# Softcap attention and soft mixture of experts on one core: 24 instead of 13 joined tanhs, 95 instead of 93 tiles of exponentials on VectorE, and the work of each period placed anew

## The chip, the cores and the metric

The kernel runs on one core of one Trainium2 chip. The metric is the device time of one execution in microseconds (us), of which three runs are given. A profile of one execution gives start and length of each instruction on five engines: TensorE (PE, with its weight loads as PEld), VectorE (DVE), ScalarE (ACT), GpSimd (POOL) and SyncE (SP). Each engine executes its own list of instructions in order; between engines, semaphores hold an instruction back until what it needs is there.

## The reference

An attention with capped scores feeds a soft mixture of experts. Batch 8, 12 heads, 448 tokens, head size 64; 8 experts with 4 slots each, 1024 hidden units.

```python
scores = cap * np.tanh(q @ k.T / sqrt(64) / cap)          # cap = 30
attn = np.exp(scores - scores.max(-1)); attn /= attn.sum(-1)
x = (attn @ v)  ->  (3584, 768)
logits = x @ phi                                          # 3584 x 32
slot_input = softmax(logits, over tokens).T @ x           # 32 x 768
slot_out[e] = relu(slot_input[e] @ w1[e]) @ w2[e]
out = softmax(logits, over slots) @ slot_out
```

## The kernel before

The scores of two heads of a batch (a "pair", `pr` in the code, 48 in all) are worked off in 7 tiles of 448 queries by 64 keys of each head, the two heads one above the other in the 128 partitions. The 336 tiles go through the kernel in 56 chunks of 6 tiles. The main loop has one period `j` for each chunk (`for j in range(NCH)`).

- **Scores** (`qk_chunk`): TensorE writes three tiles, a half chunk, into three PSUM banks with 12 small matmuls in two groups of 6.
- **Tanh** (`tanh_chunk`): ScalarE reads scores from PSUM and writes 16-bit values into the buffer `ex` of the chunk (five of them, taken in turn). Usually one instruction takes three tiles (L366), so each half of the score buffer is free again as soon as its own tanh has ended. For a period in the list `JOINED`, one instruction takes all six tiles (L362). TensorE then can't write the scores of the next chunk before all of it has ended; so in such a period `qk_chunk(2j+2)` stands behind the products of the period, not among them.
- **Exponential** (`exp_chunk`): ScalarE turns the tanhs of the chunk before into exponentials (L374). In the chunks of the dictionary `SHARED`, the first one to three tiles are done by VectorE instead: `poly_exp` computes them in seven steps, numbered 0 to 6 (L602, L604 to L609; the steps 2, 4 and 5 have two operands in memory). The table `POLY` says in which period, and at which of its places, each step of each chunk stands.
- **Products** (`pv_first`, `pv_tail`, `pv_rest`): in period `j`, TensorE multiplies the exponentials of a pair that ends in chunk `j-2` with the values, and VectorE divides by the sums (`norm`: L634 `rec`, L637 `xq`). There is one PSUM bank for them (pool `psV`).
- **Side work**: queries and keys of four heads are loaded by GpSimd's queue (`load`), transposed by TensorE (`transp`) and copied to SBUF by VectorE (L281); finished rows are transposed (`x_transp`) and copied (L689). Logits, their exponentials, slot sums and transposes follow for each batch (`logits`, `e_exp`, `slot_sums`, `e_transp`, `e_sums`). All these transposes and sums use the one PSUM buffer of the pool `psT`: a transpose waits until VectorE has copied out the one before. GpSimd also builds the block of values (`vcast`, L289) and issues the loads of the expert weights.

Within a period the places are called 0, m, e, a, b, r, c and d, each with a place just ahead (`<a`) and just behind (`>a`). The helper `at(j, place, function, ...)` books a piece of work, and `run(j, place)` emits it there. `WHEN` holds the places of the side work. Before, it has 22 entries, each with an offset in periods from the start of a batch (`PER` = 7 periods), so that all batches run alike.

After the last period come the exponentials of the last chunk, the last two pairs with their transposes (`TAILSEQ`), and then the experts (`layer1`, `layer2`) and the output.

Of the kernel before, what the change touches and what calls it, by code (L numbers as in the profile page):

```python
# [37 lines left out]
def kernel(  # L38
# [337 lines left out]
    def exp_chunk(j):  # L376
# [4 lines left out]
    JOINED = (10, 14, 17, 21, 24, 28, 29, 31, 35, 38, 42, 45, 49)  # L381
    SHARED = {1: (2, 0), 3: (3, 0), 4: (3, 0), 6: (2, 0), 7: (3, 0), 9: (3, 0), 11: (3, 0), 12: (3, 0), 14: (3, 0), 16: (3, 0), 18: (3, 0), 19: (3, 0), 21: (3, 0), 23: (3, 0), 25: (3, 0), 26: (3, 0), 28: (3, 0), 30: (3, 0), 32: (3, 0), 33: (3, 0), 35: (3, 0), 37: (3, 0), 39: (3, 0), 40: (3, 0), 42: (3, 0), 44: (3, 0), 46: (3, 0), 47: (2, 0), 48: (2, 0), 49: (3, 0), 51: (2, 0), 52: (1, 0), 53: (3, 0), 54: (1, 0)}
    POLY = {(1, 'm'): ((1, 0),),
            (1, 'e'): ((1, 1),),
            (1, '>a'): ((1, 2),),
            (1, '>b'): ((1, 3),),
            (1, '>d'): ((1, 4),),
            (2, 'r'): ((1, 5),),
            (3, 'e'): ((3, 0),),
            (3, '<a'): ((3, 1), (1, 6)),  # L390
            (3, '<b'): ((3, 2),),
            (3, '>c'): ((3, 3),),
            (4, '<a'): ((3, 4),),
            (4, '>a'): ((3, 5),),
            (4, '<c'): ((4, 0),),
            (5, 'e'): ((4, 1), (3, 6)),
            (5, '<a'): ((4, 2),),
            (5, '>b'): ((4, 3),),
            (5, '>c'): ((4, 4),),
            (6, 'e'): ((6, 0), (4, 5), (6, 1)),  # L400
            (6, '<a'): ((4, 6),),
            (6, '>d'): ((6, 2),),
            (7, 'm'): ((6, 3),),
            (7, 'e'): ((7, 0),),
            (7, '>a'): ((6, 4),),
            (7, '<b'): ((6, 5),),
            (7, '<d'): ((7, 1),),
            (8, '0'): ((7, 2), (7, 3)),
            (8, '>b'): ((6, 6), (7, 4)),
            (8, '>c'): ((7, 5),),  # L410
            (9, 'm'): ((9, 0),),
            (9, '<a'): ((7, 6),),
            (9, '>b'): ((9, 1),),
            (9, '>d'): ((9, 2),),
            (10, 'e'): ((9, 3),),
            (10, '>b'): ((9, 4),),
            (10, '>d'): ((9, 5),),
            (11, 'e'): ((11, 0),),
            (11, '<a'): ((9, 6),),
            (11, '>a'): ((11, 1),),  # L420
            (11, '>b'): ((11, 2),),
            (11, '<c'): ((11, 3),),
            (11, '>c'): ((11, 4),),
            (12, '<a'): ((12, 0),),
            (12, '<b'): ((11, 5),),
            (12, '<c'): ((12, 1),),
            (12, '>d'): ((11, 6),),
            (13, '<b'): ((12, 2),),
            (13, '>b'): ((12, 3),),
            (13, '>c'): ((12, 4),),  # L430
            (13, '>d'): ((12, 5),),
            (14, '<a'): ((14, 0), (12, 6), (14, 1)),
            (14, '<d'): ((14, 2), (14, 3)),
            (15, '>a'): ((14, 4),),
            (15, '>d'): ((14, 5),),
            (16, 'm'): ((14, 6),),
            (16, 'e'): ((16, 0),),
            (16, '<b'): ((16, 1),),
            (16, '>d'): ((16, 2),),
            (17, 'm'): ((16, 3),),  # L440
            (17, '<a'): ((16, 4),),
            (17, '>d'): ((16, 5),),
            (18, 'e'): ((18, 0),),
            (18, '>a'): ((16, 6), (18, 1)),
            (18, '>b'): ((18, 2),),
            (19, '0'): ((18, 3), (18, 4)),
            (19, 'e'): ((18, 5),),
            (19, '<a'): ((19, 0),),
            (19, '<c'): ((18, 6),),
            (19, '>c'): ((19, 1), (19, 2)),  # L450
            (20, '>b'): ((19, 3),),
            (20, '>d'): ((19, 4),),
            (21, '>a'): ((19, 5), (19, 6)),
            (21, '<b'): ((21, 0), (21, 1)),
            (21, '>c'): ((21, 2),),
            (21, '<d'): ((21, 3),),
            (22, '>b'): ((21, 4),),
            (22, '<d'): ((21, 5),),
            (23, 'm'): ((21, 6),),
            (23, '<a'): ((23, 0),),  # L460
            (23, '>a'): ((23, 1),),
            (23, '>d'): ((23, 2),),
            (24, 'e'): ((23, 3), (23, 4)),
            (24, '>d'): ((23, 5),),
            (25, 'm'): ((23, 6),),
            (25, '<a'): ((25, 0), (25, 1)),
            (25, '>b'): ((25, 2),),
            (25, '<c'): ((25, 3),),
            (25, '>d'): ((25, 4),),
            (26, '0'): ((25, 5),),  # L470
            (26, '<b'): ((25, 6),),
            (26, '<c'): ((26, 0),),
            (26, '>d'): ((26, 1),),
            (27, '>a'): ((26, 2),),
            (27, '>b'): ((26, 3), (26, 4)),
            (28, 'e'): ((26, 5), (28, 0)),
            (28, '<a'): ((26, 6),),
            (28, '>b'): ((28, 1),),
            (28, '>c'): ((28, 2),),
            (29, '>a'): ((28, 3),),  # L480
            (29, '<b'): ((28, 4),),
            (29, '>d'): ((28, 5),),
            (30, 'm'): ((28, 6),),
            (30, '>a'): ((30, 0),),
            (30, '>c'): ((30, 1),),
            (31, '0'): ((30, 2),),
            (31, 'm'): ((30, 3),),
            (31, '<b'): ((30, 4),),
            (31, '<c'): ((30, 5),),
            (32, 'e'): ((32, 0),),  # L490
            (32, '<b'): ((30, 6), (32, 1)),
            (32, '>b'): ((32, 2),),
            (32, '<c'): ((32, 3),),
            (32, '>c'): ((32, 4),),
            (33, 'e'): ((33, 0),),
            (33, '<b'): ((32, 5),),
            (33, '<c'): ((33, 1),),
            (34, '0'): ((33, 2),),
            (34, 'e'): ((33, 3),),
            (34, 'r'): ((33, 4),),  # L500
            (34, '<c'): ((32, 6),),
            (35, '0'): ((33, 5),),
            (35, '<a'): ((33, 6),),
            (35, '<b'): ((35, 0),),
            (35, '>b'): ((35, 1),),
            (35, '<c'): ((35, 2),),
            (36, '<a'): ((35, 3),),
            (36, '>a'): ((35, 4),),
            (37, 'm'): ((35, 5), (35, 6)),
            (37, 'e'): ((37, 0),),  # L510
            (37, '<a'): ((37, 1),),
            (38, 'm'): ((37, 2),),
            (38, '>a'): ((37, 3),),
            (38, '>b'): ((37, 4),),
            (38, '>c'): ((37, 5),),
            (39, 'e'): ((37, 6),),
            (39, '>a'): ((39, 0), (39, 1)),
            (39, '>b'): ((39, 2),),
            (39, '<c'): ((39, 3),),
            (39, '>c'): ((39, 4),),  # L520
            (40, 'e'): ((40, 0),),
            (40, '<b'): ((40, 1),),
            (40, '>b'): ((39, 5),),
            (40, '>c'): ((40, 2),),
            (41, '<b'): ((40, 3),),
            (41, 'r'): ((40, 4),),
            (41, '<d'): ((39, 6),),
            (42, 'm'): ((40, 5),),
            (42, '<a'): ((42, 0),),
            (42, '>a'): ((40, 6), (42, 1)),  # L530
            (43, 'e'): ((42, 2), (42, 3)),
# [284 lines left out]
    for b in range(B):  # L816
        j, p = b * PER, 6 * b

        def when(nm):
            return j + WHEN[nm][0], WHEN[nm][1]  # L820

# [413 lines left out]
```

## Time and profile before

| what | value |
|---|---|
| time, median of 3 runs | 281.53 us (281.47 to 281.86) |
| span of the profiled execution | 279.2 us |
| median time less that span | 2.3 us |
| PE busy | 247.0 us, 88% |
| DVE busy | 239.1 us, 86% |
| ACT busy | 248.6 us, 89% |
| POOL busy | 142.0 us, 51% |
| granted TensorE clock, mean | 0.985 |

The page names no separate time for the profiled execution; only its span is given. The median stands 2.3 us above it. A row of a timeline gives start, length, engine, line and operation, output and inputs, shapes and count; in brackets stands the idle time of the engine ahead of it and what ended that. ScalarE and VectorE overlap the end of one instruction with the start of the next, so the step from one start to the next start tells what an instruction costs. The last period begins at 228.4 us, the experts at 239.6 us, and the last store ends with the span.

### The profile page before, as it was taken

The page shows a single profiled execution, that of the slowest core. Times are in us where ns is not written, and L with a number is a line of the kernel's source. Part 1 is how long each engine was busy: PE and PEld are TensorE (multiplying, and loading weights), DVE is VectorE, ACT ScalarE, POOL GpSimd, SP SyncE. Part 2 cuts the span into 40 slices and gives each one's busy share as a digit, 9 for nine tenths or more (in the row PEclk, how much of TensorE's full clock was granted, in tenths as well). Part 3 has the DMA queues.
Part 4 walks back from the last instruction along what each step waited for, and adds up shares of the span by engine and source line. Part 5 has one row for each costly group of instructions (what it writes and reads, how often), then busy time and mean ns, then how long its engine had stood idle before and what let it go on. Part 6 is the DMA issues. An engine that isn't in the chain of part 4 may idle for free.

```text
span 279.2 us, 10421 instructions
## 1 busy us (share of the span) xinstructions
PE 247.0 (88%) x4560; PEld 166.6 (60%) x4560; DVE 239.1 (86%) x473; ACT 248.6 (89%) x195; POOL 142.0 (51%) x198
## 2 busy tenths in 40 slices
PE   8898989998999999989999999899999999998720
PEld 7555556756675766566756675657566678553300
DVE  3479999999999999999999999999999997347940
ACT  4999999999999999999999999999999998237720
POOL 8796548662957296728673758375743230200000
PEclk9999999999999999999999999999999999999995
DMA  6999999999999999999999999999999588979997
GB/s 197 277 193 202 219 219 234 229 221 219 224 225 220 219 229 226 225 217 229 223 226 212 213 219 231 218 210 215 231 217 215 117 279 293 367 290 383 434 424 312
DMA packets 57340, 68.08 MB, mean 244 GB/s; under 512 B 4048, under 2 KB 53840, under 8 KB 56784
## 3 DMA queue, kind: packets, MB, share of 16 engines
q0 software_dynamic: 42448, 35.31, 80.0%
q1 hardware_dynamic: 14704, 32.02, 32.6%
q8 instruction: 35, 0.57, 0.7%
q10 hardware_dynamic: 144, 0.10, 0.1%
q14 instruction: 9, 0.07, 0.1%
HBM read 91.72 MB, written 19.27 MB: 398 GB/s over the span
## 4 chain that ended last, share of the span: by engine, by line
ACT 38%; DVE 27%; PE 27%; issue 3%; POOL 1%; ACTq 0%; DVEq 0%
ACT ex L366 15%; ACT ex L374 15%; PE pv L627 8%; ACT ex L362 6%; DVE xq L637 4%; PE sc L349 3%; DVE xp L605 3%; DVE xp L607 3%; DVE ex L608 2%; DVE ex L602 2%; PE so_ps L1098 2%; PE hp L1070 2%; DVE xf L604 2%; DVE ex L609 2%; DVE xp L606 2%
## 5 line engine op out<-in xcount | busy, mean ns | idle before, releaser
L366 ACT ACTIVATE ex<-sc 128x1344 f16<-128x1344 f32 (+1 forms) x87 | 112.9, 1402 | 0.9 <-PE sc L349 0.9
L374 ACT ACTIVATE ex<-ex 128x1344 bf16<-128x1344 f16 (+5 forms) x58 | 110.7, 1916 | 0.1
L627 PE MATMUL pv<-vbd,ex 128*128 128x130 bf16 (+1 forms) x1610 | 94.0, 212 | 7.6 <-POOL vbd L289 3.4
L627 PEld LDWEIGHTS <-ex 128*128 128x128 bf16 (+1 forms) x1680 | 75.6, 101 | 34.9 <-issue 6.2
L289 POOL CAST vbd<-vraw 64x896 bf16<-64x896 f32 x46 | 47.3, 1028 | 57.3 <-PE pv L627 35.7
L349 PE MATMUL sc<-qT,kT 64*64 64x448 bf16 x672 | 66.0, 359 | 6.7 <-ACT ex L366 4.8
L362 ACT ACTIVATE ex<-sc 128x2688 f16<-128x2688 f32 x13 | 33.6, 2586 | 0.0
L349 PEld LDWEIGHTS <-kT 64*64 64x64 bf16 x672 | 22.1, 105 | 16.3 <-ACT ex L366 6.9
L637 DVE TENSOR_TENSOR xq<-pv,rec 128x448 bf16<-128x448 f32 x46 | 28.7, 625 | 1.6
L607 DVE TENSOR_TENSOR xp<-xp,xf 128x1344 f16<-128x1344 f16 (+2 forms) x34 | 27.1, 798 | 0.6
L608 DVE TENSOR_TENSOR ex<-ex,xp 128x1344 uint16<-128x1344 uint16 (+2 forms) x34 | 26.9, 791 | 0.2
L605 DVE TENSOR_TENSOR xp<-xf 128x1344 f16<-128x1344 uint16 (+2 forms) x34 | 26.8, 789 | 0.2
L116 POOL DMA_DIRECT2D w1b<-in_moe_w_dram x32 | 26.3, 825 | 0.0
L602 DVE TENSOR_SCALAR ex<-ex 128x1344 uint16<-128x1344 f16 (+2 forms) x34 | 17.0, 500 | 1.4 <-ACT ex L366 0.8
L606 DVE TENSOR_SCALAR xp<-xp 128x1344 f16<-128x1344 f16 (+2 forms) x34 | 17.2, 505 | 0.6
L281 DVE COPY kT<-kps 128x896 bf16<-128x896 bf16 x23 | 14.2, 617 | 4.0 <-PE kps L276 2.8
L297 POOL MEMSET vbd<- 64x1 bf16 x22 | 2.8, 129 | 28.6 <-PE pv L627 28.3
L604 DVE TENSOR_SCALAR xf<-ex 128x1344 uint16<-128x1344 uint16 (+2 forms) x34 | 16.7, 491 | 0.4
L185 POOL DMA_DIRECT2D qb<-in_q_dram x22 | 16.3, 740 | 1.2 <-PE qps L279 0.5
L609 DVE TENSOR_SCALAR ex<-ex 128x1344 uint16<-128x1344 uint16 (+2 forms) x34 | 16.4, 483 | 0.4
L120 POOL DMA_DIRECT2D w2d<-in_moe_w_dram x21 | 16.4, 816 | 0.0
L185 POOL DMA_DIRECT2D kb<-in_k_dram x22 | 16.3, 739 | 0.0
(124 smaller groups left out, 320.2 us busy)
## 6 DMA issues: line engine op xcount, KB each, us to landing
w1b<-in_moe_w_dram POOLq DMA_DIRECT2D x32, 384.0 KB, 10.2
vraw<-in_v_dram SPq DMA_DIRECT2D x44, 224.0 KB, 6.2
w2d<-in_moe_w_dram POOLq DMA_DIRECT2D x21, 384.0 KB, 9.9
w2t<-w2d SPq DMA_DIRECT2D x21, 384.0 KB, 6.2
qb<-in_q_dram POOLq DMA_DIRECT2D x22, 224.0 KB, 8.2
kb<-in_k_dram POOLq DMA_DIRECT2D x22, 224.0 KB, 8.1
w2b<-in_moe_w_dram POOLq DMA_DIRECT2D x11, 384.0 KB, 9.5
out_dram<-ob SPq DMA_DIRECT2D x2, 1536.0 KB, 7.7
```

What stands on the lines that cost most here:

```text
L116: pool.dma_start(out=w1b[e][:, js, fs], in_=w1r[:, e, js, fs])
L185: pool.dma_start(out=t, in_=quad_ap(nm, Q))
L289: pool.tensor_copy(vbds[Q % 2][r, :, :, c0:c0 + DH], raw[r])
L349: ins = pe.matmul(sc[cs, u, 0:S], qkT["k", Q][r, c, cs], qkT["q", Q][r, :, cs], start=True, stop=True).ins
L362: apart["t", i - 1] = apart["t", i] = act.activation(exs[j].bitcast(F16), own["board"][:, :, 0:S], ACT.Tanh, scale=qk_scale / cap).ins
L366: ins = act.activation(exs[j][:, half * CS + u0:half * CS + u1, :].bitcast(F16), (own[0] if i == u0 == 0 else sc)[:, u0:u1, 0:S], ACT.Tanh ...
L374: act.activation(exs[j][:, u0:u1, :], exs[j][:, u0:u1, :].bitcast(F16), ACT.Exp, scale=cap)
L605: lambda: dve.tensor_tensor(p, s, s.bitcast(F16), op=ALU.mult),
L607: lambda: dve.tensor_tensor(p, p, s, op=ALU.mult),
L608: lambda: dve.tensor_tensor(y, y, p, op=ALU.add),
L627: pe.matmul(out_, exs[j][r, u, q0:q0 + (HP if tail else P)], v_, start=(c == 0 and g == gs[0] < NF), stop=(c == NT - 1), skip_group_check= ...
L637: dve.tensor_tensor(xq[Q][:, h, s0:s1, :], pv[:, 0:s1 - s0, 0:DH], rec.to_broadcast([P, s1 - s0, DH]), op=ALU.mult)
```

## The change

Four tables are replaced, and the loop that books the side work reads the new one. Nothing else is edited; the amount of work on TensorE stays, and so do the fill-in matmuls.

- `JOINED` has 24 periods instead of 13. The first is 5 instead of 10.
- `SHARED` has 34 chunks as before. Chunks 1, 52 and 54 have one tile more on VectorE (3, 2 and 2), chunk 39 one less (2), and chunk 45 takes the place of chunk 46. That makes 95 tiles instead of 93.
- `POLY` places almost all of the 238 steps anew.
- `WHEN` has an entry for each load, transpose, copy, logit and sum of each batch, without a common pattern.

```diff
-    JOINED = (10, 14, 17, 21, 24, 28, 29, 31, 35, 38, 42, 45, 49)
-    SHARED = {1: (2, 0), 3: (3, 0), 4: (3, 0), 6: (2, 0),
...
+    JOINED = (5, 7, 8, 10, 12, 14, 16, 17, 19, 21, 22, 24, 26, 28, 29, 31, 33, 35, 36, 38, 42, 43, 45, 49)
+    SHARED = {1: (3, 0), 3: (3, 0), 4: (3, 0), 6: (2, 0),
...
-            (54, '<b'): ((54, 0), (53, 5)),
-            (54, '>b'): ((54, 1),),
-            (54, '>c'): ((53, 6),),
-            (55, '0'): ((54, 2),),
-            (55, 'e'): ((54, 3),),
...
+            (54, '<c'): ((54, 2), (53, 6)),
+            (54, '>c'): ((54, 3), (54, 4)),
+            (55, 'm'): ((54, 5),),
+            (55, '<a'): ((54, 6),)}
...
-    WHEN = {'k1': (0, 'm'), 'q1': (0, 'b'), 'v1': (3, 'c'), 'k2': (2, 'a'), 'q2': (2, 'd'), 'v2': (7, 'b'),
...
+    WHEN = {'k1': (1, '0'), 'q1': (1, '0'), 'lk2': (2, 'c'), 'lq2': (0, 'e'), 'k2': (2, 'b'), 'q2': (1, 'd'),
...
+            'q23': (52, '0'), 'x21': (54, 'd')}
...
-        for n in (2, 3):
-            quad_in(3 * b + n, *(when(f"{x}{n}") for x in ("lk", "lq", "k", "q", "v")))
+        for Q in range(max(3 * b + 1, 2), min(3 * b + 4, NQ)):
+            quad_in(Q, *(WHEN.get(f"{x}{Q}", (NCH - 1, "e")) for x in ("lk", "lq", "k", "q")), None)
...
-            at(*when(f"x{hq}"), x_transp, NQB * b + hq)
+            at(*WHEN[f"x{NQB * b + hq}"], x_transp, NQB * b + hq)
```

The diff makes the new kernel's line numbers in these functions two lower (L689 becomes L687) and those behind the tables 13 higher (L1070 becomes L1083).

**ScalarE, chunks 1 to 7.** Each `ex<-sc` is a tanh, of three tiles (128x1344) or joined (128x2688), each `ex<-ex` an exponential; a minus stands for before, a plus for the change:

```order
 L366 ACTIVATE ex<-sc 128x1344 x2
-L374 ACTIVATE ex<-ex 128x1792
+L374 ACTIVATE ex<-ex 128x1344
 L366 ACTIVATE ex<-sc 128x1344 x4
 L374 ACTIVATE ex<-ex 128x2688
 L366 ACTIVATE ex<-sc 128x1344 x2
 L374 ACTIVATE ex<-ex 128x1344
-L366 ACTIVATE ex<-sc 128x1344 x2
+L362 ACTIVATE ex<-sc 128x2688
 L374 ACTIVATE ex<-ex 128x1344
 L366 ACTIVATE ex<-sc 128x1344 x2
 L374 ACTIVATE ex<-ex 128x2688
```

The exponentials of chunk 1 lose a tile to VectorE, and the tanh of chunk 5 is one instruction instead of two.

**VectorE, end of period 54 and period 55, before.** `ex_5289` is chunk 53, `ex_5394` chunk 54; `xps_5462` holds the transposed rows of pairs 42 and 43, `xps_5505` those of pair 44:

```order
L634 RECIPROCAL rec_5456<-pv_5399 128x7
L637 TENSOR_TENSOR xq_5398<-pv_5399,rec_5456 128x448
L689 COPY xT_5461<-xps_5462 128x896
L609 TENSOR_SCALAR ex_5289<-ex_5289 128x1344
L605 TENSOR_TENSOR xp_155<-xf_154 128x448
L606 TENSOR_SCALAR xp_155<-xp_155 128x448
L607 TENSOR_TENSOR xp_155<-xp_155,xf_154 128x448
L689 COPY xT_5504<-xps_5505 128x448
L608 TENSOR_TENSOR ex_5394<-ex_5394,xp_155 128x448
L609 TENSOR_SCALAR ex_5394<-ex_5394 128x448
L634 RECIPROCAL rec_5537<-pv_5490 128x7
L637 TENSOR_TENSOR xq_5398<-pv_5490,rec_5537 128x448
```

**The same place with the change.** Here `ex_5268` is chunk 53, `ex_5338` chunk 54, `xps_5452` the pairs 42 and 43, and `xps_5486` pair 44:

```order
L632 RECIPROCAL rec_5435<-pv_5380 128x7
L635 TENSOR_TENSOR xq_5379<-pv_5380,rec_5435 128x448
L603 TENSOR_TENSOR xp_155<-xf_154 128x896
L607 TENSOR_SCALAR ex_5268<-ex_5268 128x1344
L604 TENSOR_SCALAR xp_155<-xp_155 128x896
L605 TENSOR_TENSOR xp_155<-xp_155,xf_154 128x896
L687 COPY xT_5451<-xps_5452 128x896
L606 TENSOR_TENSOR ex_5338<-ex_5338,xp_155 128x896
L607 TENSOR_SCALAR ex_5338<-ex_5338 128x896
L687 COPY xT_5485<-xps_5486 128x448
L632 RECIPROCAL rec_5516<-pv_5471 128x7
L635 TENSOR_TENSOR xq_5379<-pv_5471,rec_5516 128x448
```

The copy of the pairs 42 and 43 stood right behind `xq` and now stands behind four steps of exponentials; the steps of chunk 54 have two tiles instead of one.

More of the change, by code (lines that the diff above doesn't have):

```diff
@@ L490 @@
[L490 to L499 removed]
+            (26, 'e'): ((25, 5),),
+            (26, '>b'): ((26, 0),),
+            (26, '<d'): ((26, 1),),
+            (27, 'm'): ((26, 2), (26, 3)),
@@ L572 @@
[L572 to L583 removed]
+            (40, 'm'): ((39, 4), (40, 0)),
```

359 lines of the change are left out of this document (179 added, 180 removed), and 25 rows, old and new, of the table WHEN.

## The prediction

> **What bounds the kernel now.** I read the page first, then the busy time by stretches of the main loop, then the timelines of ScalarE, TensorE and VectorE where they meet.
>
> ```profile
> span 279.2 us, 10421 instructions
> PE 247.0 (88%) x4560; PEld 166.6 (60%) x4560; DVE 239.1 (86%) x473; ACT 248.6 (89%) x195; POOL 142.0 (51%) x198
> ...
> 20.00:205.00 185.00, 171.19 (x3396) 118.38 (x3396) 177.89 (x339) 184.99 (x131) 115.59 (x155) 1.00 1.24 221
> 205.00:230.00 25.00, 23.46 (x456) 16.64 (x453) 24.54 (x57) 25.00 (x20) 7.67 (x11) 1.00 0.94 204
> ```
>
> The columns of a stretch are PE, PEld, DVE, ACT and POOL. ScalarE is busy for 184.99 of 185 us: the main loop goes at its pace. VectorE follows closely: 7.1 us free of 185, and 0.46 of the last 25. TensorE has 13.8 us free. So a microsecond taken from ScalarE is a microsecond gained only as long as VectorE and TensorE keep up, and only if the work behind the loop starts earlier too.
>
> ScalarE's prices are read from the steps between starts:
>
> ```profile
> 86.51 2.69 ACT L366 ACTIVATE ex<-sc 128x1344 f16<-128x1344 f32 x2
> 88.85 1.56 ACT L374 ACTIVATE ex<-ex 128x1344 bf16<-128x1344 f16 x1
> 90.06 2.65 ACT L362 ACTIVATE ex<-sc 128x2688 f16<-128x2688 f32 x1
> 92.35 2.69 ACT L374 ACTIVATE ex<-ex 128x2688 bf16<-128x2688 f16 x1
> 94.69 1.53 ACT L366 ACTIVATE ex<-sc 128x1344 f16<-128x1344 f32 x1
> ```
>
> Two tanhs of three tiles take 88.85 - 86.51 = 2.34 us, a joined one 92.35 - 90.06 = 2.29. Exponentials of three tiles take 1.21, of six 2.34, so a tile costs 0.375.
>
> **The change part by part.** *Joined tanhs.* Eleven more at 2.34 - 2.29 = 0.05 us each take 0.55 us off ScalarE. [...]
>
> *Tiles.* Up to the start of the last period VectorE takes one tile more (chunk 1 and 52 one more each, 39 one less; 45 for 46 is even), which takes 0.375 us off ScalarE. The other one, of chunk 54, is saved inside the last period. So ScalarE would begin the last period 0.55 + 0.375 = 0.92 us earlier.
>
> *Waits of ScalarE.* A joined tanh keeps all six banks. TensorE can write them again only after its end, and whatever is late on TensorE ahead of these matmuls delays the next tanh.
>
> ```profile
> 118.41 2.73 ACT L362 ACTIVATE ex<-sc 128x2688 f16<-128x2688 f32 x1
> 120.70 2.77 ACT L374 ACTIVATE ex<-ex 128x2688 bf16<-128x2688 f16 x1
> 123.33 2.44 ACT L362 ACTIVATE ex<-sc 128x2688 f16<-128x2688 f32 x1
> ...
> 206.26 2.03 ACT L374 ACTIVATE ex<-ex 128x1792 bf16<-128x1792 f16 x1
> 208.18 2.48 ACT L366 ACTIVATE ex<-sc 128x1344 f16<-128x1344 f32 x2
> ...
> 105.66 0.76 PE L349 MATMUL sc<-qT,kT 64*64 64x448 bf16 x12 [0.28 <-ACT ex L362]
> ```
>
> The engine counts as busy there, but the steps are too long: 123.33 - 120.70 = 2.63 instead of 2.34, and 208.18 - 206.26 = 1.92 instead of 1.21 + 0.375 = 1.59. So two of the 13 joined periods (28 and 49) cost 0.29 and 0.33, or 0.05 each over all 13. The last row, from period 24, shows why the others cost nothing: TensorE's 12 matmuls take 0.76 us, and the exponential beside them lasts 1.21. Eleven more at 0.05 add 0.53. Against that, in the order of the new kernel, the late steps of periods 28 and 49 stand earlier on VectorE (the last steps of chunk 26 at the head of period 28; the copy of the queries at the head of 49), which can take away up to 0.62. I put the sum at nothing; its ends are -0.62 and, if each new one costs 0.31, +3.4 us.
>
> *VectorE's load.* By form, with mean ns behind the busy time:
>
> ```profile
> L605 DVE TENSOR_TENSOR xp<-xf 128x896 f16<-128x896 uint16 x5 | 3.1, 617 | 0.1
> L606 DVE TENSOR_SCALAR xp<-xp 128x896 f16<-128x896 f16 x5 | 2.0, 404 | 0.1
> L605 DVE TENSOR_TENSOR xp<-xf 128x448 f16<-128x448 uint16 x2 | 0.8, 389 | 0.0
> L606 DVE TENSOR_SCALAR xp<-xp 128x448 f16<-128x448 f16 x2 | 0.5, 274 | 0.0
> ```
>
> Three of the seven steps are like L605 (+0.23 for a second tile), four like L606 (+0.13): 1.2 us a tile, 2.4 for two. In the order, 75 steps instead of 63 stand right behind the step of the same chunk that they need. Such a step starts after the end of that one, others about 0.09 before it (rows of the tail below: 231.90 + 0.38, then 232.31; but 229.07 + 0.62, then 229.61). That is 12 x 0.1 = 1.2 us more, 3.6 in all. Over most of the loop the 7.1 us free take it in, as I see it, since what is added is spread; where it can't is the end.
>
> *The end.* First TensorE, then VectorE:
>
> ```profile
> 230.14 0.90 PE L627 MATMUL pv<-vbd,ex 128*128 128x130 bf16 x12
> 230.88 0.33 PE L675 MATMUL xps<-ident,xq 128*128 128x128 bf16 x3
> 231.14 0.22 PE L680 MATMUL xps<-ident,xq 64*64 64x64 bf16 x2
> 231.19 1.12 PE L627 MATMUL pv<-vbd,ex 64*64 64x65 bf16 x23
> 232.25 1.43 PE L627 MATMUL pvm<-vbd,ex 128*128 128x130 bf16 x21
> ```
>
> ```profile
> 229.07 0.62 DVE L637 TENSOR_TENSOR xq<-pv,rec 128x448 bf16<-128x448 f32 x1
> 229.61 0.61 DVE L689 COPY xT<-xps 128x896 bf16<-128x896 bf16 x1
> 230.14 0.50 DVE L609 TENSOR_SCALAR ex<-ex 128x1344 uint16<-128x1344 uint16 x1
> 230.55 0.39 DVE L605 TENSOR_TENSOR xp<-xf 128x448 f16<-128x448 uint16 x1
> ...
> 231.90 0.38 DVE L608 TENSOR_TENSOR ex<-ex,xp 128x448 uint16<-128x448 uint16 x1
> 232.31 0.28 DVE L609 TENSOR_SCALAR ex<-ex 128x448 uint16<-128x448 uint16 x1
> 232.50 0.20 DVE L634 RECIPROCAL rec<-pv 128x7 f32<-128x7 f32 x1
> 232.74 0.62 DVE L637 TENSOR_TENSOR xq<-pv,rec 128x448 bf16<-128x448 f32 x1
> 234.15 0.39 DVE L689 COPY xT<-xps 128x448 bf16<-128x448 bf16 x1 [0.79 <-PE xps L680]
> ```
>
> TensorE's transposes at 230.88 go into the one buffer `xps`, which the copy at 229.61 frees at 230.22. They do not wait. Now four steps stand ahead of that copy. By the means above, less the overlap of about 0.09: step 2 of two tiles 0.54; the last step of chunk 53 (230.55 - 230.14) 0.41; step 3, 0.31; step 4, directly behind it, 0.64. The sum is 1.90. The copy would end at 230.22 + 1.90 = 232.12, and the transposes would start at 232.2 instead of 230.88: 1.3 us late, with all products of the last three pairs queued behind them on TensorE. VectorE would moreover come to this place later. Chunk 52 costs it 1.2 us more there and ScalarE 0.375 less, so it can be up to 1.6 us behind its old place; it has 0.46 free in that stretch, but period 50 has been emptied for it (two steps of exponentials instead of six). I take 0.4. The sum at the end is 1.7 us, with ends of 0 (TensorE's queue can make it up) and 1.3 + 1.6 = 2.9. TensorE's rows from 230.14 on follow without a gap, so I see no room to make it up.
>
> *Loads.* One row of the loads that were moved matters:
>
> ```profile
> kb<-in_k_dram POOLq DMA_DIRECT2D x22, 224.0 KB, 8.1
> ```
>
> The load of the keys of pairs 40 and 41 is issued some 0.7 us into period 42 and needed some 3 us into 43. Period 42 lasts 2.29 + 2.34 us, so the load has about 6.9 us, while one takes 8.1. TensorE may stand for 1.2 us there. The scores of period 44 are issued ahead of it, and that period gives ScalarE 2.34 + 2.34 us of work, so I count nothing; without that cover it would be 1.2. The start gains the tile of chunk 1, and its transposes stay behind their loads.
>
> *Sum.* -0.92 + 0 + 1.7 = +0.8 us. The profiled span of 279.2 would become 280.0. The median of the runs lies 2.3 us above the span; with that the time is 281.5 + 0.8 = **282.3 us**.
>
> **The rivals.** *The end makes it up (faster).* If VectorE reaches the last two periods with time in hand, or TensorE has the slack, the 0.92 us is kept, 280.6 us; with both old waits gone, 280.0. For it speaks that ScalarE has been the pace everywhere; against it, TensorE's gapless rows from 230 us on. [...]
>
> *VectorE becomes the bound of the loop (slower).* It needs 3.6 us more in a loop that is to be 0.92 shorter, 4.5 of the 7.1 free. Part of what is free lies in waits that stay, for sums and transposes. It decides from the point where less than 4.5 can be used. With half, 3.5, the loop is 0.1 longer instead of 0.92 shorter, and with 1.7 at the end the time is 283.3.
>
> *Joined tanhs without cover (slower).* Each of the eleven waits as in period 28 or 49, 0.31 us: +3.4, 285.7; if half do, 284.0. Against it, 11 of 13 cost nothing, and in the order the joined periods that follow each other mostly have exponentials of six tiles between them. [...]
>
> That the change does not do what it says is out: the order has 24 joined tanhs.
>
> **How the numbers follow.** A measurement of this kernel can tell 0.2%, 0.56 us, from no change. My forecast has a chance of 0.50; its own range is 281.6 to 283.2 (the end between 1.0 and 2.6), of which slower holds 0.30, within 0.2% 0.17 and faster 0.03. The end made up has 0.25: 0.20 faster, 0.05 within. VectorE as the bound has 0.17: 0.14 slower, 0.03 within. Joined tanhs without cover have 0.08, all slower. Together: faster 0.23, within 0.25, slower 0.52. The range reaches from 280.3 to 283.8: it leaves out the lower half of the first rival and nearly all of the last.
>
> **What would show it.** Right: ScalarE's last period begins about 0.9 us earlier than at 228.4, and TensorE's transposes of pair 44 wait over a microsecond for the copy of VectorE. Wrong at the end: these transposes do not wait, and the experts begin earlier than at 239.6. Wrong in the loop: steps of ScalarE that are longer than 1.17, 1.21, 2.29 and 2.34 by more than 0.6 us in sum; behind joined tanhs it is the third rival, with VectorE free for under 3 us of the loop the second.

## The result, and the profile after

| | before | changed |
|---|---|---|
| median of the runs | 281.5 us (281.35 to 281.86) | 291.48 us (290.22 to 292.07) |
| ratio | 1 | 1.0344 [1.0319, 1.0369] |
| profiled execution: span, clock | 279.2 us, 0.985 | 290.3 us, 0.968 |

Ratios here leave out executions over 1.5% slower than the fastest of the same kernel: two of the four of `e3_when_old` (its ratio stands for 293.3 us), one of the ten of `cast_before` and one of the ten of `r_all` (354.2 us). The prediction said 282.3 us, 280.3 to 283.8: the direction was right, the size far too small. The head of the page and two stretches of the main loop, with the columns PE, PEld, DVE, ACT, POOL and the granted clock behind them:

```profile
span 290.3 us, 10404 instructions
PE 250.3 (86%) x4560; PEld 170.3 (59%) x4560; DVE 246.9 (85%) x473; ACT 248.1 (85%) x184; POOL 139.4 (48%) x198
...
20.00:205.00 185.00, 167.88 (x3311) 117.84 (x3311) 175.46 (x327) 179.88 (x117) 107.40 (x148) 0.98 1.21 213
205.00:236.50 31.50, 28.32 (x548) 19.59 (x545) 30.52 (x67) 30.98 (x24) 12.17 (x18) 1.00 0.97 193
```

ScalarE, never idle before, now stands for 5.1 of 185 us, while VectorE is busy for less of the stretch than before (175.46 for 177.89): no engine is full. The clock's 0.98 is new; it was 1.00. A period begins here with the start of its first tanh. Counted so, the loss falls on few places (us):

| from, to | before | changed | difference |
|---|---|---|---|
| to period 0 | 6.14 | 6.33 | +0.19 |
| period 0 to 6 | 23.13 | 26.03 | +2.90 |
| 6 to 12 | 25.38 | 25.08 | -0.30 |
| 12 to 13 | 3.56 | 5.65 | +2.09 |
| 13 to 33 | 81.65 | 81.89 | +0.24 |
| 33 to 34 | 3.56 | 4.41 | +0.85 |
| 34 to 55 | 84.95 | 85.54 | +0.59 |
| 55 to the experts | 11.26 | 15.77 | +4.51 |

The rest of the span (39.6 us) is unchanged; the sum is 11.1, the difference of the spans. ScalarE's two longest waits, in its timeline after:

```profile
25.34 1.34 ACT L374 ACTIVATE ex<-ex 128x1344 bf16<-128x1344 f16 x1
28.48 2.41 ACT L362 ACTIVATE ex<-sc 128x2688 f16<-128x2688 f32 x1 [1.81 <-PE sc L349]
...
59.73 1.40 ACT L374 ACTIVATE ex<-ex 128x1344 bf16<-128x1344 f16 x1
63.09 1.29 ACT L366 ACTIVATE ex<-sc 128x1344 f16<-128x1344 f32 x1 [1.96 <-PE sc L349]
```

It waits for scores of TensorE. Behind the second wait stands VectorE: TensorE in turn waits 1.18 us for `xq`. Here are VectorE's rows with GpSimd's cast of the values in the same microseconds, first after, then before. L603 and L605 are the same step (2, of chunk 11) at the same place of the order, ahead of `rec` and `xq` of the pair:

```profile
55.60 0.62 DVE L281 COPY kT<-kps 128x896 bf16<-128x896 bf16 x1
56.13 1.60 DVE L603 TENSOR_TENSOR xp<-xf 128x1344 f16<-128x1344 uint16 x1
57.65 0.19 DVE L632 RECIPROCAL rec<-pv 128x7 f32<-128x7 f32 x1
57.88 0.62 DVE L635 TENSOR_TENSOR xq<-pv,rec 128x448 bf16<-128x448 f32 x1
...
56.09 0.93 POOL L289 CAST vbd<-vraw 64x896 bf16<-64x896 f32 x1 [2.80 <-PE pv L625]
...
58.65 0.84 PE L625 MATMUL pv<-vbd,ex 128*128 128x130 bf16 x12 [1.18 <-DVE xq L635]
```

```profile
53.26 0.85 DVE L605 TENSOR_TENSOR xp<-xf 128x1344 f16<-128x1344 uint16 x1
54.03 0.20 DVE L634 RECIPROCAL rec<-pv 128x7 f32<-128x7 f32 x1
54.26 0.62 DVE L637 TENSOR_TENSOR xq<-pv,rec 128x448 bf16<-128x448 f32 x1
...
53.63 1.26 POOL L289 CAST vbd<-vraw 64x896 bf16<-64x896 f32 x1 [2.24 <-PE pv L627]
```

Before, the step begins 0.37 us ahead of the cast: it takes 0.85, and the cast takes 1.26. After, it begins 0.04 us behind the start of the cast, takes 1.60 and ends 0.71 behind the cast's end; `rec`, `xq` and TensorE's next products come 0.75 us later for it. In these rows the one that began later took longer: the cast before (1.26 instead of 0.93), the step after (1.60 instead of 0.85).

Call a step overlong if it takes over 0.1 us more than the median of its form. There are 9 such steps before with 2.1 us in sum, and 21 after with 6.8. Of these, 1 before (0.2 us) and 8 after (4.0 us) stand beside a cast; all others are steps with one input (TENSOR_SCALAR) that began while GpSimd was issuing a DMA, at most 0.41 us over each. Of the five longest after, those at 16.3, 56.1, 144.0 and 236.2 us stand ahead of the four losses of the table (start, period 12, period 33, end); the fifth (120.4 us) is ahead of a wait of 0.3 us in period 28, which was there before as well. At the start and the end the runs below find further causes.

The clock: three stretches of 3.41 us ran at half clock. Each is shown behind the stretch ahead of it:

```profile
22.31:25.72 3.41, 1.57 (x29) 1.02 (x26) 3.21 (x7) 3.41 (x4) 0.10 (x1) 1.00 1.25 205
25.72:29.13 3.41, 3.41 (x41) 1.95 (x35) 1.60 (x4) 1.60 (x2) 0.92 (x1) 0.50 1.25 205
56.44:59.85 3.41, 2.23 (x64) 2.02 (x60) 3.38 (x6) 3.41 (x3) 3.41 (x5) 1.00 1.20 234
59.85:63.27 3.42, 3.42 (x55) 2.24 (x51) 2.38 (x6) 1.46 (x3) 1.16 (x3) 0.50 1.22 231
237.35:240.76 3.41, 1.41 (x16) 0.98 (x16) 3.34 (x8) 3.41 (x4) 0.00 (x0) 1.00 0.85 290
240.76:244.17 3.41, 3.41 (x43) 2.98 (x41) 1.83 (x5) 0.73 (x2) 0.00 (x0) 0.50 0.52 149
```

TensorE was busy for 1.57, 2.23 and 1.41 of 3.41 us, and then ran at half its clock for 3.41 us. The kernel before has no such stretch until 271 us, near its end, where the changed kernel has one too.

The end, in the timelines of VectorE, TensorE and GpSimd (these answer to the prediction's last two blocks):

```profile
236.17 1.15 DVE L602 TENSOR_SCALAR xf<-ex 128x896 uint16<-128x896 uint16 x1
237.24 0.19 DVE L632 RECIPROCAL rec<-pv 128x7 f32<-128x7 f32 x1
237.46 0.62 DVE L635 TENSOR_TENSOR xq<-pv,rec 128x448 bf16<-128x448 f32 x1
238.00 0.61 DVE L603 TENSOR_TENSOR xp<-xf 128x896 f16<-128x896 uint16 x1
238.53 0.50 DVE L607 TENSOR_SCALAR ex<-ex 128x1344 uint16<-128x1344 uint16 x1
238.95 0.39 DVE L604 TENSOR_SCALAR xp<-xp 128x896 f16<-128x896 f16 x1
239.37 0.63 DVE L605 TENSOR_TENSOR xp<-xp,xf 128x896 f16<-128x896 f16 x1
239.91 0.62 DVE L687 COPY xT<-xps 128x896 bf16<-128x896 bf16 x1
...
238.14 0.34 PE L889 MATMUL junk<-ones 128*128 128x384 bf16 x1 [1.23 <-DVE xq L635]
240.59 0.35 PE L673 MATMUL xps<-ident,xq 128*128 128x128 bf16 x3 [1.15 <-DVE xT L687]
240.94 1.80 PE L625 MATMUL pv<-vbd,ex 64*64 64x65 bf16 x23
...
235.79 1.28 POOL L289 CAST vbd<-vraw 64x896 bf16<-64x896 f32 x1
```

L602 takes 1.15 us beside the cast (0.39 is its median), `xq` starts 2.53 us behind the period's start (before: 0.70), the four steps stand ahead of the copy, and the products behind run at half clock (23 take 1.80 us, before 1.12).

### The profile page after: what moved, and what is told of

Same layout as the page of the kernel before. It is cut to its first block, busy times and chain, and to the rows that moved or that the text cites. A ratio compares the mean times of both kernels' runs of the same rounds, so it can differ in the third digit from the quotient of the medians.

```text
span 290.3 us, 10404 instructions
## 1 busy us (share of the span) xinstructions
PE 250.3 (86%) x4560; PEld 170.3 (59%) x4560; DVE 246.9 (85%) x473; ACT 248.1 (85%) x184; POOL 139.4 (48%) x198
## 4 chain that ended last, share of the span: by engine, by line
DVE 49%; PE 31%; ACT 13%; issue 3%; POOL 1%; ACTq 0%; DVEq 0%
PE pv L625 9%; DVE xq L635 7%; DVE xp L603 6%; DVE xp L605 6%; DVE ex L606 5%; PE sc L349 4%; ACT ex L362 4%; DVE xf L602 4%; ACT ex L366 4%; ACT ex L374 3%; DVE xp L604 3%; DVE ex L600 3%; DVE qT L281 3%; DVE ex L607 3%; DVE kT L281 3%
## 5 line engine op out<-in xcount | busy, mean ns | idle before, releaser
L374 ACT ACTIVATE ex<-ex 128x1344 bf16<-128x1344 f16 (+4 forms) x58 | 104.6, 1808 | 0.1
L366 ACT ACTIVATE ex<-sc 128x1344 f16<-128x1344 f32 (+1 forms) x65 | 81.6, 1315 | 5.6 <-PE sc L349 5.5
L362 ACT ACTIVATE ex<-sc 128x2688 f16<-128x2688 f32 x24 | 59.0, 2459 | 1.9 <-PE sc L349 1.8
L603 DVE TENSOR_TENSOR xp<-xf 128x1344 f16<-128x1344 uint16 (+1 forms) x34 | 29.0, 853 | 0.3
L605 DVE TENSOR_TENSOR xp<-xp,xf 128x1344 f16<-128x1344 f16 (+1 forms) x34 | 28.1, 825 | 0.4
L606 DVE TENSOR_TENSOR ex<-ex,xp 128x1344 uint16<-128x1344 uint16 (+1 forms) x34 | 27.6, 812 | 0.3
L602 DVE TENSOR_SCALAR xf<-ex 128x1344 uint16<-128x1344 uint16 (+1 forms) x34 | 18.8, 552 | 0.5
L607 DVE TENSOR_SCALAR ex<-ex 128x1344 uint16<-128x1344 uint16 (+1 forms) x34 | 17.6, 517 | 0.6
L604 DVE TENSOR_SCALAR xp<-xp 128x1344 f16<-128x1344 f16 (+1 forms) x34 | 17.4, 513 | 0.6
L185 POOL DMA_DIRECT2D kb<-in_k_dram x22 | 16.3, 740 | 2.8 <-PE kps L279 2.8
L600 DVE TENSOR_SCALAR ex<-ex 128x1344 uint16<-128x1344 f16 (+1 forms) x34 | 16.7, 491 | 0.5 <-ACT ex L362 0.3
L687 DVE COPY xT<-xps 128x896 bf16<-128x896 bf16 (+1 forms) x24 | 14.4, 598 | 1.7 <-PE xps L678 1.6
```

The costliest lines, as they stand in the source:

```text
L185: pool.dma_start(out=t, in_=quad_ap(nm, Q))
L362: apart["t", i - 1] = apart["t", i] = act.activation(exs[j].bitcast(F16), own["board"][:, :, 0:S], ACT.Tanh, scale=qk_scale / cap).ins
L366: ins = act.activation(exs[j][:, half * CS + u0:half * CS + u1, :].bitcast(F16), (own[0] if i == u0 == 0 else sc)[:, u0:u1, 0:S], ACT.Tanh ...
L374: act.activation(exs[j][:, u0:u1, :], exs[j][:, u0:u1, :].bitcast(F16), ACT.Exp, scale=cap)
L603: lambda: dve.tensor_tensor(p, s, s.bitcast(F16), op=ALU.mult),
L605: lambda: dve.tensor_tensor(p, p, s, op=ALU.mult),
```

## Experiments

Theories: A, VectorE hands over late at three places, by the order of its steps; B, the eleven joined tanhs themselves; C, the two tiles; D, the side work. After four runs came E: the lateness arises where a step meets GpSimd's cast. ScalarE's waits are summed as in the prediction: steps from start to start over 1.17 (half of the 2.34 for two tanhs), 1.21, 2.29 and 2.34 us.

| kernel | median us | ratio to before |
|---|---|---|
| e1_joined13 | 292.29 | 1.0362 [1.0334, 1.0390] |
| e2_tiles93 | 289.25 | 1.0261 [1.0236, 1.0286] |
| e3_when_old | 296.27 | 1.0419 [1.0358, 1.0481] |
| e4_joined24 | 294.98 | 1.0473 [1.0437, 1.0508] |
| cast_after | 287.38 | 1.0222 [1.0134, 1.0311] |
| cast_before | 281.73 | 1.0011 [0.9983, 1.0039] |
| r_start | 289.25 | 1.0256 [1.0205, 1.0308] |
| r_end | 288.50 | 1.0244 [1.0194, 1.0295] |
| m_three | 287.79 | 1.0212 [1.0169, 1.0254] |
| f_fill | 294.73 | 1.0444 [1.0393, 1.0495] |
| r_all | 282.34 | 1.0009 [0.9982, 1.0035] |
| m_end | 284.39 | 1.0111 [1.0072, 1.0150] |
| e7_entry | 288.65 | 1.0244 [1.0208, 1.0280] |
| r_best | 283.09 | 1.0055 [1.0036, 1.0073] |
| r_new7 | 283.42 | 1.0071 [1.0044, 1.0098] |
| r_new10 | 282.95 | 1.0048 [1.0030, 1.0066] |

**One table at a time.**

e1 is the changed kernel with the old list of joined tanhs, e4 the kernel before with the new one:

```diff
-    JOINED = (5, 7, 8, 10, 12, 14, 16, 17, 19, 21, 22, 24, 26, 28, 29, 31, 33, 35, 36, 38, 42, 43, 45, 49)
+    JOINED = (10, 14, 17, 21, 24, 28, 29, 31, 35, 38, 42, 45, 49)
```

e2 changes four entries of `SHARED`, e3 takes all of `WHEN` from the kernel before, of which two entries here:

```diff
-    1: (3, 0)   39: (2, 0)   52: (2, 0)   54: (2, 0)
+    1: (2, 0)   39: (3, 0)   52: (1, 0)   54: (1, 0)
...
-    'x0': (6, 'a'), 'x21': (54, 'd')
+    'x0': (5, 'c'), 'x21': (54, 'c')
```

> The changed kernel with the old list of 13 joined tanhs; tiles, steps of VectorE and side work stay new. Theory A (VectorE hands over late at three places: start, period 12, end; TensorE then has holes, its clock is halved, ScalarE waits): only the entry into the joint score board at period 5 goes (its wait is 1.9 of 8.5 us); period 12 is no longer joined and waits less, the end keeps its 4.5 us: 287 to 290 us. Theory B (the eleven joined tanhs themselves cost the time): the waits of ScalarE fall from 8.5 to about 1 us, 7.5 less, and 0.55 comes back for the lost joinings: 284 to 285 us.

> The changed kernel with the old numbers of tiles (chunk 1 two, 39 three, 52 and 54 one): 93 in all. Theory C (two more tiles are too much for VectorE): 283 to 285 us. Theory A: the end gains about 1 us, since two steps ahead of the late copy work on one tile and not two, while the start and period 12 stay: 289.5 to 291.5 us.

> The changed kernel with chunk loads, transposes and sums at the places of before; joined tanhs, tiles and the order of VectorE's steps stay new. Theory D (the side work was placed badly): 283 to 285 us. Theory A (the order of VectorE's steps against rec and xq makes it late): 289 to 293 us, with TensorE's clock still halved at least once in the loop, and the transposes of pair 44 still over 2 us late.

> The kernel before with the new list of 24 joined tanhs alone; everything else stays old. Theory B (the eleven joined tanhs themselves): +7 us, 288 to 289 us. Theory A: eleven joinings gain 0.55 us, the entry at period 5 costs up to 1.9: 281 to 283 us, with no halved clock at period 12 and the last period to the experts as before (11.3 us).

B falls: without the eleven joinings the time does not come down, and ScalarE's waits are still 7.8 us (8.5 in the changed kernel), partly at other periods (13 and 20). But the same joinings in the old kernel cost 13.5 us, with 16.5 us of waits from period 4 on and three stretches of 6.83 us at half clock. C and D fall as well, as causes that stand alone. A is near for e2 (0.25 us under its range) and e3 (293.3 us by its ratio, 0.3 over) and wrong for e1 and e4. So no table is shown to be bad by itself. The tables were made for each other, and the mixtures e1, e3 and e4 lose at new places. That asked for a cause below the tables, which the overlong steps gave.

**GpSimd's cast.**

```diff
-        pool.tensor_copy(vbds[Q % 2][r, :, :, c0:c0 + DH], raw[r])
+        cols = slice(0, 1 if Q > 1 else NT)
+        pool.tensor_copy(vbds[Q % 2][r, :, cols, c0:c0 + DH], raw[r][:, :, cols, :])
```

> The changed kernel with the values' cast on GpSimd cut to one of its seven tiles from the third quad on (the other six keep old values; this work is left out); its waits and its place in GpSimd's queue stay. Theory E (VectorE's steps are stretched while GpSimd casts beside them: 21 steps over their median by 6.8 us in sum, among them those at 16.3, 56.1, 144.0 and 236.2 us, right ahead of ScalarE's longest waits): the stretch falls under 4 us, the holes of period 12 and of the end shrink, and the time is 284 to 287 us; the start's stretch (16.3) stays, since the first casts are whole. Theory A (the order of the steps alone makes the hand-overs late): 289.5 to 291.5 us.

> The same cut of the cast in the kernel before, as the control: its stretches are 2.1 us in sum, nearly none of them beside a cast. All theories: 280.8 to 281.6 us. A clearly lower time would mean that the cut takes something else away.

Both kernels leave out six of the seven tiles of the cast from the third quad (four heads) on; they serve only to measure. The control did not move (281.73 us, 0.1 over its range, with a ratio of 1.0011). Its overlong steps even rose from 2.1 to 4.4 us, nearly all beside issues of DMAs: such a step costs nothing where no engine waits for it. In the changed kernel the overlong steps fell to 3.8 us, the waits from 8.5 to 3.3, those of periods 12 and 33 to 0.15 and 0.20, with the order of the steps as it was.

The median is 0.4 over the range, because the four runs fall into two pairs: spans of 283.7 and 283.9 us at a mean clock of 0.986, and of 287.3 and 287.6 at 0.974. The difference of the clocks, 0.012 of 285.6 us, is 3.4 us of clock or two stretches of 3.41 us at half; the pairs differ by 3.65. So a halved stretch would cost about 1.8 us, an estimate: only one execution, of the shorter pair, has a trace. Traces with and without a halved stretch at the same place differ a little less. The waits of periods 4 and 5 are 2.3 us in the changed kernel and 1.0 in `m_three`, whose tables are the same there, without it; that of period 33 is 0.9 us in the changed kernel and, with it, 2.3 in `r_end`.

**Three entries moved, nothing undone.**

```diff
-            (11, '>b'): ((11, 2),),
+            (11, '<c'): ((11, 2),),
-            (32, '>b'): ((32, 2),),
+            (32, '<c'): ((32, 2),),
-    'lq13': (26, 'b')
+    'lq13': (26, 'c')
```

> The changed kernel with three entries moved and nothing undone: step 2 of chunk 11 and step 2 of chunk 32 go from ahead of the pair's rec and xq to behind them, and the load of the queries of quad 14 goes behind GpSimd's cast of period 26. Theory E (a step of VectorE that begins while GpSimd casts is held up, and rec and xq with it): the stretches at 56.1, 120.4 and 144.0 us go (0.75, 0.78 and 0.46 us), ScalarE's waits of periods 12, 28 and 33 (2.15, 0.44 and 0.90 us) fall under 0.8 us in sum, no halved clock near 60 us: 287.5 to 289 us. Rival (VectorE's load alone makes it late, wherever its steps stand): the waits turn up in the next periods, 290.5 to 292 us.

Period 12's place in the trace of this run (L450 is the step, VectorE first, then GpSimd):

```profile
53.85 0.62 DVE L281 COPY kT<-kps 128x896 bf16<-128x896 bf16 x1
54.39 0.20 DVE L479 RECIPROCAL rec<-pv 128x7 f32<-128x7 f32 x1
54.62 0.62 DVE L482 TENSOR_TENSOR xq<-pv,rec 128x448 bf16<-128x448 f32 x1
55.16 0.85 DVE L450 TENSOR_TENSOR xp<-xf 128x1344 f16<-128x1344 uint16 x1
...
54.34 0.92 POOL L289 CAST vbd<-vraw 64x896 bf16<-64x896 f32 x1 [2.79 <-PE pv L472]
```

`rec` and `xq`, which read PSUM, run beside the cast at their usual 0.20 and 0.62; the step follows at 0.85. The waits of periods 12, 28 and 33 fell from 3.4 to 0.3 us, no stretch was halved before the last period, and 3.7 us came back with all 24 joinings and 95 tiles in place.

Part of that sum is luck. Between the two profiles, 3.6 us came back from period 12 to 34, 3.1 of them in the waits of the three edited periods, and 1.8 at the start, where nothing was edited (no stretch was halved there this time). At the end 1.1 were lost; there 6.83 us instead of 3.41 were halved. This run takes the two steps both out of the cast and from ahead of `xq`, so by itself it does not tell E from A. `cast_after` keeps the order and takes only the cast away, and the same waits go. The two together show E for periods 12 and 33.

**The start and the end.** From the first joined period to the last, the scores stand in one buffer of six banks, the joint board of the texts below; ahead of it there are two of three. The cover of a tanh is the work that ScalarE still has while TensorE writes its scores. In r_start the first nine periods, in r_end the steps from period 53 on, are those of the kernel before; e7_entry drops one joining; m_end is m_three with another order of the last steps.

r_start and e7_entry, and one of the steps that r_start also takes over:

```diff
-    JOINED = (5, 7, 8, 10, 12, 14, 16, 17, 19, 21, 22, 24, 26, 28, 29, 31, 33, 35, 36, 38, 42, 43, 45, 49)
+    JOINED = (10, 12, 14, 16, 17, 19, 21, 22, 24, 26, 28, 29, 31, 33, 35, 36, 38, 42, 43, 45, 49)
...
-            (3, 'r'): ((3, 3),),
+            (3, '>c'): ((3, 3),),
```

```diff
-    JOINED = (5, 7, 8, 10, 12, 14, 16, 17, 19, 21, 22, 24, 26, 28, 29, 31, 33, 35, 36, 38, 42, 43, 45, 49)
+    JOINED = (7, 8, 10, 12, 14, 16, 17, 19, 21, 22, 24, 26, 28, 29, 31, 33, 35, 36, 38, 42, 43, 45, 49)
```

Of r_end, then of m_end, the main entries in period 54 and the last one:

```diff
-            (54, '0'): ((53, 3), (53, 4)),
-            (54, 'm'): ((54, 0),),
-            (54, '>a'): ((54, 1),),
-            (54, '<c'): ((54, 2), (53, 6)),
+            (54, '<a'): ((53, 4),),
+            (54, '<b'): ((54, 0), (53, 5)),
+            (54, '>b'): ((54, 1),),
+            (54, '>c'): ((53, 6),),
+            (55, '0'): ((54, 2),),
```

```diff
-            (54, '>a'): ((54, 1),),
-            (54, '<c'): ((54, 2), (53, 6)),
-            (54, '>c'): ((54, 3), (54, 4)),
+            (54, '>c'): ((53, 6),),
+            (55, '0'): ((54, 1), (54, 2)),
+            (55, 'm'): ((54, 3),),
+            (55, 'e'): ((54, 4),),
...
-    'x21': (54, 'd')
+    'x21': (54, 'c')
```

> The changed kernel with the first nine periods as before: joint score board from period 10 on (the joinings of 5, 7 and 8 gone), steps of VectorE up to period 8, two tiles of chunk 1, loads and transposes of quads 2 to 4 as before. If the loss at the start is local (3.3 us of ScalarE's waits in periods 2 to 5, the first halved clock), it goes and 0.53 us of gains go with it: 288.5 to 289.5 us, with the waits of period 12 and of the end unchanged. If every period shifts the next ones (no local causes), anything else: 286 or less, or 291 and more.

> The changed kernel with the end as before: VectorE's steps from period 53 on, one tile of chunk 54, the transposes of pair 42 and the sums of batch 6 at their old places; chunk 52 keeps two tiles. If the end's loss is local: from the start of the last period to the experts 11.3 to 11.8 us instead of 15.8, no halved clock there, and 4.5 - 0.4 us less in all: 286.5 to 288 us. If VectorE comes to the end late by its load, only the four steps ahead of the copy go (1.9 us): 289 to 290 us.

> The changed kernel without the joining of period 5, so that the joint score board is entered at period 7, where the exponential behind the tanhs of period 6 has six tiles; all else stays new. If the wait at the entry comes from the short cover (an exponential of three tiles): ScalarE's waits of periods 4 to 7 fall from 2.3 to under 0.5 us and the first halved clock goes, 289.5 to 290.5 us in all. If it comes from VectorE's late xq of the start: 1 us or more of waits stays in periods 3 to 7, 291 to 292 us.

> The three moved entries of before, and in addition the last steps of VectorE and the transposes of pair 42 in another order, with the same tiles (two each of chunks 52 and 54): step 1 of chunk 54 no longer between the end of the products of values and rec (where it meets GpSimd's cast), no steps of chunk 54 ahead of the copy that frees xps. If the end is lost by this order: from the start of the last period to the experts 12 to 12.5 us instead of 16.8, no halved clock at the end, 283 to 284.5 us. If it is lost by VectorE's load (two tiles more in the last four chunks): the steps are only late at another place, 286 to 288 us.

The start: with the entry into the joint board at period 7, the waits of periods 4 to 7 fell from 2.3 us to none and the first halved stretch went; waits of 0.85 stayed in periods 2 and 3. The cover decides: at period 5 only an exponential of three tiles (1.21 us) stands behind the tanhs of period 4, at period 7 one of six. At the entry the board takes the banks of both old buffers, so even the first scores wait until both tanhs of period 4 have ended. With products between their two groups, TensorE is at them from 25.51 to 28.43 us; in the row of period 24 in the prediction they took 0.76. Without the halved stretch the entry at period 5 costs 1.0 us (m_three), with it 2.3. The gain of 2.8 us was larger than expected, since the wait of period 12 also fell from 2.15 to 1.02 (no halved stretch there in this run). r_start gives nearly the same, within its range.

The end: r_end takes 12.2 us to the experts (11.3 to 11.8 expected) without a halved stretch there; that it is 0.5 us over its range goes with a halved stretch that now stands at period 33 of its profile. m_end is within its range, by 0.1 us, and tells order from load: with the same tiles it takes 3.4 us less than m_three. From the last period to the experts it takes 13.3 us instead of 16.8, not the 12 to 12.5 expected:

```profile
231.03 0.19 DVE L479 RECIPROCAL rec<-pv 128x7 f32<-128x7 f32 x1
231.25 0.62 DVE L482 TENSOR_TENSOR xq<-pv,rec 128x448 bf16<-128x448 f32 x1
231.79 0.61 DVE L534 COPY xT<-xps 128x896 bf16<-128x896 bf16 x1
...
236.02 1.03 PE L472 MATMUL pvm<-vbd,ex 128*128 128x130 bf16 x15 [1.07 <-DVE ex L454]
```

`xq` starts 1.47 us behind the period's start and the copy directly behind it; TensorE now waits 1.07 us for the last step of chunk 54 with its two tiles. r_end, with one tile there, takes 1.1 us less, so that part of the loss looks like load; no run changes the tile alone in this order.

**Filling the holes.** Small products of no use are put into TensorE's holes. The question is whether the time follows the clock (286.5 to 289 us if it stays full more often) or not (290.5 to 292).

```diff
-    at(34, "<b", fill, 7)
+    [at(*x) for x in ((34, "<b", fill, 7), (4, "e", fill, 25), (12, "e", fill, 30), (33, "e", fill, 25), (54, "<d", fill, 25), (55, "<a", fill, 30))]
```

> The changed kernel with 25 to 30 more small products of no use (128 x 57, some 0.03 us each) on TensorE at five places: ahead of the products of values of periods 4, 12 and 33, and ahead of the transposes of pairs 42 and 44 at the end. They run where TensorE stands waiting for xq anyway (0.84, 1.18, 0.91, 1.23 and 1.15 us). [...] Rival (the clock is only an effect and costs nothing): 290.5 to 292 us.

It failed, and not as a test of the clock: the small products wait for `xq` themselves and stand behind the hole instead of in it.

```profile
57.16 0.96 PE L655 MATMUL pv<-ones 128*128 128x57 bf16 x30 [1.03 <-DVE xq L635]
```

They add their 0.96 us to the lateness: 294.7, over both ranges. One thing it does show: in its profile no stretch is halved before the last period, and ScalarE still waits for 8.5 us. The late hand-overs cost time without the clock; the halved clock comes on top (about 1.8 us a stretch, by the estimate from `cast_after`).

**All repairs together.** r_all joins r_start, m_three and the end of the kernel before from period 52 on; it has 21 joinings and 93 tiles. r_best, r_new7 and r_new10 go on from it; r_new7 moreover takes back the changed kernel's start with the board from period 7 (23 joinings, 94 tiles). The edits that are new in r_best, of which the last two keep the moved entry of period 49, then some that the last two add:

```diff
-            (40, '>c'): ((40, 3),),
+            (41, 'a'): ((40, 3),),
-            (49, 'm'): ((48, 2),),
-            (49, 'e'): ((48, 3), (47, 6)),
+            (49, 'm'): ((47, 6), (48, 2)),
+            (49, 'e'): ((48, 3),),
-    'x19': (50, 'a'), 'x20': (52, 'a')
+    'x19': (50, 'c'), 'x20': (52, 'b')
```

```diff
-            (49, '<d'): ((48, 5), (49, 2)),
+            (49, '<d'): ((48, 5), (48, 6), (49, 2)),
-            (51, '<b'): ((49, 5), (51, 1), (49, 6), (51, 2)),
+            (51, '<b'): ((49, 5), (49, 6), (51, 1), (51, 2)),
-    'x15': (41, 'e')
+    'x15': (40, 'c')
```

> The repairs together: the start of the kernel before (first nine periods), the three moved entries, the end of the kernel before from period 52 on, three tiles of chunk 39; in between the changed kernel with 21 joined tanhs. If the losses are local: no halved clock, ScalarE's waits 1 to 1.5 us as before, 0.4 us of joinings kept, 280.8 to 282 us. If the rest of the new order loses too (collisions that move with the phase): 284 us and more.

> All repairs with what the run before left: the kernel before's order from period 50 on (logits of batch 6 came 0.35 us late), step 3 of chunk 40 behind the copy of xT (ScalarE waited 0.37 us in period 42), the last step of chunk 47 one place earlier (0.30 us in period 49). 93 tiles, 21 joined tanhs. If these waits are local: the last period begins 0.8 to 1.2 us earlier than in the run before, 280.8 to 281.4 us, faster than both kernels by 0.1 to 0.4%. If they only move: 281.6 to 282.4 us.

> All repairs, second try: the changed kernel's start with the joint score board from period 7 (23 joined tanhs, 94 tiles), the three moved entries, the end of the kernel before from period 52; in addition the last steps of chunks 47, 48 and 49 one place earlier, and the transposes of pair 30 at their old place. If what the segments of the earlier runs gained adds up: ScalarE needs 0.3 us less from period 0 to 14 than in the kernel before, the end costs 0.1 to 0.6 more, 280.6 to 281.6 us. If the new phase makes VectorE meet GpSimd's casts at new places: 282 to 285 us.

> The same with the start of the kernel before (board from period 10, 21 joined tanhs, 93 tiles): as the run with all repairs, less its waits at periods 42, 49 and 53 (0.37, 0.30 and 0.52 us): 281.0 to 281.8 us if they go, 282.3 if they only move.

r_all is level with the kernel before (0.3 us over its range): the losses are local. The three runs that went on from there missed their ranges by 1.2 to 1.8 us, and none beats the kernel before; each made something late elsewhere. In r_best the sums `wps` now stand behind a transpose and wait 1.32 us for its copy; in r_new10 the periods 52 and 53 take 9.54 us instead of the 8.39 before. TensorE's row of r_best, and ScalarE's wait for the logits of batch 6 in r_all, which is 0.77 us in the three that follow it:

```profile
215.28 0.31 PE L588 MATMUL wps<-ones,ET 128*128 128x1 bf16 x7 [1.32 <-DVE xT L535]
```

```profile
222.11 0.28 ACT L559 ACTIVATE E<-lps 128x128 bf16<-128x128 f32 x1 [0.35 <-PE lps L543]
```

## Why the prediction was wrong, by its steps

- *Joined tanhs, 0.05 us each*: right. They take 2.29 us in the new trace too, and between periods 14 and 20, with two more of them, ScalarE needs 24.64 us in m_three instead of 24.75.
- *Waits of ScalarE, "nothing"*: this step failed. They rose by 7.3 us (1.15 to 8.46), over the upper end of 3.4; less the 0.92 forecast as gain, that is the 6.4 us by which the loop up to the start of the last period grew. The rows of periods 28 and 49 were taken as the price of a joining. m_three, with all 24 joinings, has waits of 3.0 us, so most of them are not the joinings'. The entry at period 5 is the one joining that the runs show without cover, and the prediction had not asked where the board is entered: it took the cover from period 24, well inside the joint board.
- *VectorE's load is taken in by its free time*: the load was (m_end keeps all of it), the place of the steps was not. Every step was priced by its mean (0.31 to 0.64 us for the four of the tail), which was true of the old order, where what stood beside the casts was nearly always `rec`, `xq` or a copy from PSUM. In the changed kernel five of the six steps that began in the first half of a cast took 0.46 to 0.78 us more (the sixth, at 197.48 us, kept its 0.50, and the cast took 1.32 instead of 0.93), and where such a step stood ahead of `xq`, `xq` was late (by 0.75 us in period 12). GpSimd's casts were in none of the sums.
- *The end, 1.7 us*: the part of the four steps, 1.90 us, came out (the copy starts 2.45 us behind `xq`, before 0.54), and so did the wait of over a microsecond that was to show it (1.15 us). VectorE's lateness was 1.83 us instead of 0.4, and TensorE's clock added about 1.3 (3.64 us instead of 2.32 for the products from 240.94 on). With the 1.3 forecast for the transposes these two make 4.4 of the 4.5.
- *Loads*: right; no wait at the keys of pairs 40 and 41.
- *The rivals*: VectorE as the bound did not occur, it is busy for 175 of 185 us while everyone waits. Joined tanhs without cover named the right symptom, scores that come late, and was right at period 5; for periods 12 and 33 the cause was another, and "behind joined tanhs" could not tell the two apart.
- *The sum*: m_three gives back 3.7 us, m_end a further 3.4, e7_entry 2.8: 9.9 of the 10.0 lost. That they add up so well is in part luck, since m_three and e7_entry both gained at the start and at period 12. The three were not run as one kernel; r_all, with other repairs at the same places, gives back 9.1.

## To carry to other kernels

In a kernel whose engines are all nearly full, a new order is priced at the hand-overs: for each step put ahead of one that another engine waits for, ask what a third engine does at that moment, since a mean duration held here only for the neighbours it was measured with (step 2 of three tiles: 0.85 us, 1.60 beside a cast). Where GpSimd's cast was released by the same event, steps that read and write SBUF on VectorE were better placed behind the work from PSUM: in m_three, with two of them and one load moved, the waits of the three edited periods fell from 3.4 to 0.3 us. Tables that were tuned together are not separable: undoing one of them is no test of it.

## What the runs showed of the hardware

- VectorE beside GpSimd's cast, in the changed kernel: a step that began 0.02 to 0.38 us into a cast took 1.60 instead of 0.85, 1.29 instead of 0.51 and 1.15 instead of 0.39 us; one that began 0.59 us into it took 1.07 instead of 0.85 (179.1 us). Where the step began first, the cast took up to 1.61 instead of 0.93 (131.0 us). `rec` and `xq`, which read PSUM, took their usual 0.20 and 0.62 beside the cast of `m_three`.
- TensorE's clock was halved for 3.41 us behind stretches of 3.41 us that were far from idle: in the changed kernel TensorE was busy for 1.57, 2.23 and 1.41 us of the stretch ahead, 41 to 65%, and its longest wait there was 1.23 us. In some runs it stayed at half for a second stretch (6.83 us in all): in e4_joined24 the mean clock from 20 to 100 us was 0.87, which is about three times 6.83 us at half; in f_fill three transposes still took 0.50 instead of 0.33 us at 243.87, more than 3.41 us behind the start at 237.71.
- The three halved stretches of the changed kernel begin at 25.72, 59.85 and 240.76 us, 34.13 and 180.91 us apart, 10 and 53 times 3.413. The busy share alone does not decide. The stretch from 56.44 us on, with 2.23 us busy, was followed by half clock; the one from 271.48 us on, 72 times 3.413 us behind the first halved one, with 2.18, was followed by full clock. So was this one, 49 times 3.413 us behind it:

```profile
192.97:196.38 3.41, 2.31 (x49) 1.68 (x44) 3.34 (x7) 3.41 (x2) 1.62 (x2) 1.00 1.25 232
```

- Which hole was hit differed between the runs. r_end was halved at 145.3, behind this stretch; the changed kernel was halved at 59.9, and kept its full clock behind the wait of 0.91 us that ends at 146.3. What else decides was not shown.

```profile
141.87:145.28 3.41, 2.29 (x57) 1.93 (x52) 3.38 (x7) 3.41 (x2) 3.08 (x4) 1.00 1.27 223
```
